# Indirect scatters and gathers from GpSimd beside a bucketed attention and its MLP

## The chip, the cores and the metric

The kernel runs on one core of a Trainium2 chip. The metric is device time of one execution in microseconds (us). The kernel before takes 893.82 us (median of 2 runs, 893.76 to 893.87).

## The reference

The inputs are q, k and v of shape (4, 8, 768, 64), a projection of shape (64, 6), and the weights of an MLP. Each query and key gets a bucket from the signs of its six projections. Attention is a softmax over the keys of the same bucket; the MLP has a PReLU with one slope per hidden column.

```
q_bucket = sum over n of (q @ proj > 0)[n] * 2**n          # k_bucket likewise
scores   = where(q_bucket == k_bucket, q @ k.T / 8, -1e9)
attn     = exp(scores - max) / (sum + 1e-9)
x        = (attn @ v), heads side by side                  # 3072 x 512
h        = x @ w_in                                        # 512 -> 2048
out      = (max(h, 0) + alpha * min(h, 0)) @ w_out         # 3072 x 512
```

Nothing that the change adds is part of this computation.

## The kernel before

All of the work is done by `fast_path`. A general path stands behind a flag and doesn't run on these inputs.

**Attention.** The loop goes over 16 pairs: batch (4) times two neighbouring heads (4). A pair's q and k are loaded as tiles of 128 partitions by 6 chunks by 2 heads by 64, where a row of the sequence is 6 * partition + chunk. For each pair TensorE transposes q and k (`turn`), hashes them (`hash_bits`), computes the scores of 12 cells (`scores`; a cell is 128 keys by 384 queries of both heads), the products with v (`attend`) and the sums of the exponentials (`totals`). The hash enters the scores as a first matmul, which leaves keys of other buckets so low that their exponential vanishes. ScalarE takes each cell from PSUM through an exponential into one of six tiles `pt`. The PSUM tiles of the scores share one tag with three buffers; transposes, hashes and sums use the same tag.

`add_first` to `add_total` sum the exponentials on VectorE (accp, accd). From pair 1 on, a part of that sum is a transfer issued by GpSimd, which accumulates half of `pt` 2 into accp (L747). `divide` inverts the sums. Between its steps GpSimd copies reciprocals from one group of partitions to another (rr, L806 and L807), and VectorE puts weight work and `add_first` between, so that it need not wait for the copies.

At the end of a pair, `magnitude` squares q and k on ScalarE (L687). It writes over the tile that it reads; what is wanted is the sum of the squares. Then q and k of the pair three ahead are loaded into those tiles (three buffers each, SP's queue). On ScalarE the order is: the twelve exponentials of a pair, signs of the hash, copies of the transposes, a weight step, the square of q, the square of k, another weight step (L581), and the exponentials of the next pair.

Beside this, VectorE rounds the MLP's weights piece by piece, and SP stores them to HBM (w_in_s, w_out_r).

**MLP.** The second stage runs through the four batches. A batch has 8 blocks of the first product (`ff1`) and 7 of the second (`ff2`). Each block is a `Product`: seven half-sized products in place of eight, with sums made by VectorE. One quarter of each `ff1` block leaves PSUM by a ScalarE copy into h (L912), a tile of the pool `mid` with tag "h" and two buffers. VectorE reads h and writes g. In the first batch GpSimd also loads w_out_r, and stores sums of its parts to w_out_s (L957, L964); after that it has nothing to do until it reads the flag at the end.

**Order and waits.** The instructions of an engine keep the order in which they are written (`do` is `tc.keep_in_program_order`). The tile framework works out which instruction must wait for which: a reader for its writer, a writer for earlier readers and writers of the same tile, a tile for those that used its buffer before. DMAs signal when their data has landed.

Of the kernel before, what the change touches and what calls it, by code (L numbers as in the profile page):

```python
# [8 lines left out]
F32 = mybir.dt.float32  # L9
# [397 lines left out]
def fast_path(  # L407
# [13 lines left out]
    P = 128  # L421
    B, H, S, D = q.shape
# [5 lines left out]
    NC = S // P  # L428
# [4 lines left out]
    CW = CH * P  # L433
# [8 lines left out]
    do = tc.keep_in_program_order  # L442
    PE, DVE, ACT, POOL = nc.tensor, nc.vector, nc.scalar, nc.gpsimd

    const = ctx.enter_context(tc.tile_pool(name="const", bufs=1))
    dram = ctx.enter_context(tc.tile_pool(name="dram", bufs=1, space=bass.MemoryType.DRAM))
    mid = ctx.enter_context(tc.tile_pool(name="mid", bufs=2))
# [6 lines left out]
    NPAIR = len(pairs)  # L454
# [3 lines left out]
    ident = const.tile([P, P], F32, name="ident")  # L458
# [20 lines left out]
    nat, tr, bits = {}, {}, {}  # L479
# [18 lines left out]
            queue.dma_start(nat[name, pi][:, cs, s], src[b, 2 * hp + s].rearrange("(p c) d -> p c d", c=NC)[:, cs])  # L498

    nil = []  # L500

    def setup():

        zero = pool.tile([P, 512], BF16, name="zero", bufs=1)
        do(DVE.memset(zero, 0.0))
        do(DVE.memset(wh, 0.0))
        for s in range(2):
            nc.sync.dma_start(wh[D * s : D * s + D, :NB], proj)
        nc.sync.dma_start(alpha16, moe_alpha.rearrange("(t p) -> t p", p=P))
        make_identity(nc, ident)  # L510
        do(DVE.memset(ones, 1.0))

        ps = psum_av.tile([P, 2, 512], F32, name="nil", tag="av")
        nil.append(lambda: do(PE.matmul(ps[:, 0], zero[:, :P], zero, start=True, stop=True)))
        for i in range(7):
            nil[0]()

        do(DVE.memset(hb, 0.0))
        for r in range(0, P, 32):
            do(DVE.memset(hb[r : r + 2 * NB], 1.0 if r % D else -1.0))  # L520
            do(DVE.memset(hb[r : r + NB], -1e-37))

        do(DVE.tensor_scalar(hb_k[:, 0:1], hb, -1.0, None, op0=ALU.mult))
        do(DVE.memset(hb_k[:, 1:2], 0.0))
        for r in range(0, P, 32):
            do(DVE.memset(hb_k[r : r + 2 * NB, 1:2], 0.5))
        for t in pts:
            do(POOL.memset(t[:, :, :, CW : CW + 1], 1.0))
        for t in qbs:
            do(POOL.memset(t, 0.0))  # L530

    def setup_alpha():
        ps = two_banks("alps")[:, 0, :NF]
        do(PE.transpose(ps, alpha16, ident[:NF, :NF]))
        do(DVE.tensor_copy(alpha, ps))
# [25 lines left out]
    def load_weight(i):  # L561
        if i < NW:
            i = order[i]
            raw[i] = pool.tile([P, 512], moe_w_in.dtype, name=f"raw{i}", tag="raw", bufs=3)
            nc.sync.dma_start(raw[i], piece(i))
# [17 lines left out]
    def weight_clamp(i):  # L583
        if i < NW:
            i = order[i]
            x = wx[i]
            do(DVE.tensor_scalar(x, x, HI_MIN, None, op0=ALU.max, op1=ALU.max, accum_out=wmax[:, i : i + 1]))

    def weight_parts(i):
        i = order[i]  # L590
        lo, hi = halves(i)
        x = wx[i]
        wr[i] = r = pool.tile([P, 512], F32, name=f"wr{i}", tag="wr", bufs=1)
        do(DVE.tensor_scalar(
            x.bitcast(U32), x.bitcast(U32), 3, 0xC0000000, op0=ALU.logical_shift_left, op1=ALU.bitwise_xor,
        ))
        do(DVE.tensor_scalar(r.bitcast(U32), x.bitcast(U32), 0x7F800000, None, op0=ALU.bitwise_and))
        do(DVE.scalar_tensor_tensor(r, lo, 2.0 ** -52, r, op0=ALU.mult, op1=ALU.mult))
# [65 lines left out]
    def two_banks(name):  # L664
        return psum.tile([P, 2, 512], F32, name=name, tag="sc", bufs=3)
# [77 lines left out]
    def add_first(pi):  # L743
        accp[pi] = pool.tile([P, 2 * NCH, CW], F32, name=f"accp{pi}", tag="accp", bufs=1)
        do(DVE.tensor_tensor(accp[pi], p(0), p(1), op=ALU.add))  # L745
        if pi:
            nc.gpsimd.dma_start(accp[pi][:, 2:], p(2)[:, 2:], accum_op=ALU.add)  # L747
# [6 lines left out]
    def add_third(pi):  # L754
        n = 2 if pi else 4
        do(DVE.tensor_tensor(accp[pi][:, :n], accp[pi][:, :n], p(2)[:, :n], op=ALU.add))

    def add_total(pi):
        do(DVE.tensor_tensor(accd[pi], accd[pi], accp[pi], op=ALU.add))  # L759
# [77 lines left out]
    def sum_x(b, n, engine):  # L837

        to, a, c = ((3, 5, 0), (5, 2, 5), (4, 2, 3), (6, 4, 1))[n]
        if to != 5:  # L840
            x_m[b, to] = mid.tile([P, 2, CW], F32, name=f"x{b}_{to}", tag=f"x{to}", bufs=1)
        do(engine.tensor_tensor(x_m[b, to], x_m[b, a], x_m[b, c], op=ALU.subtract))
# [292 lines left out]
    for pi in range(NPAIR):  # L1135
        i = 2 * pi

        def weight_begin():
            weight_clamp(i)
            weight_parts(i)  # L1140
            add_first(pi)

        scores(pi, [c for c in CELLS if pi or c not in ahead])
        if pi:
            divide(pi - 1, weight_begin)
        else:
            add_first(pi)
        weight_sum(i)
        weight_group(i)
        load_weight(i + 3)  # L1150
        if pi == 0:
            weight_abs(1, DVE)
        weight_clamp(i + 1)
        add_third(pi)
        add_last(pi)
        weight_parts(i + 1)
        weight_sum(i + 1)
        weight_group(i + 1)
        load_weight(i + 4)
        add_total(pi)  # L1160
        weight_sums(2)
        if pi + 1 < NPAIR:
            hash_bits(pi + 1)
        if pi + 2 < NPAIR:
            turn(pi + 2, "q")
            turn(pi + 2, "k")
        attend(pi)
        if pi + 1 == NPAIR:
            now = ff1(0, 0)
            now.step(1)  # L1170
        totals(pi)
        if pi + 1 == NPAIR:
            now.step(5)
            divide(pi)
        else:
            weight_abs(i + 2)
        if pi + 2 < NPAIR:
            load(pi + 2, "v")
        if pi in (9, 11, 15):
            load_w((9, 11, 15).index(pi))  # L1180
        if pi in (9, 10, 12):
            load_x(0, *{9: (0,), 10: (2, 3), 12: (1,)}[pi])
        if 11 <= pi < 14 or pi == 15:
            sum_x(0, min(pi - 11, 3), DVE)
        if pi == 1:
            setup_alpha()
        for name in "qk":
            magnitude(pi, name)
            if pi + 3 < NPAIR:
                load(pi + 3, name)  # L1190
        if pi + 1 < NPAIR:
            weight_abs(i + 3)
# [10 lines left out]
    for j, (b, what, n) in enumerate(blocks):  # L1203
        n2 = n + 1 if what == "2" else 0 if n == NI - 1 else 7
        if n2 == 0:
            sides_g(b, 0)
            sum_w2(b, 0, 3, 4)
        now.step(2) if j else now.step(6)
        if j == 0:
            now.step(3)  # L1210
            now.step(7)
            now.step(2)
        now.step(22)
        if (b, what, n) == (1, "1", 1):
            largest()
        if 0 < n2 < 7:
            sides_g(b, n2)
            sum_w2(b, n2, 3, 4)
        if n2 < 7:
            sum_g2(b, n2, 3, 4)  # L1220
        if j:
            now.step(5)
            now.step(6)
            now.step(3)
            sum_w2(b, n2, 6)
            now.step(7)
            sum_w2(b, n2, 5)
            sum_g2(b, n2, 5)
        if (b, what, n) == (1, "1", 3):
            verdict()  # L1230

        for n_out in [(), (0,), (1,), (2, 3), (4,), (5, 6), (7,)][j] if j < 7 else ():
            sum_out(n_out)
        for n_out in [(1,), (2, 3), (4,), (5, 6), (7,)][j] if j < 5 else ():
            load_out(n_out)
        if what == "1":
            load_w(b * NI + n + 3)

            if 0 <= n - NI + (4 if b else 2) < 2:
                load_w2(b, n - NI + (4 if b else 2))  # L1240
        else:
            load_w2(b, n + 2)
            if b + 1 < B:
                if n == 0:
                    load_x(b + 1)
                if n == 6:
                    for m in range(4):
                        sum_x(b + 1, m, DVE)
        if j + 1 < len(blocks):
            turn_out()  # L1250
        else:
            turn_last(0)
        before = now
        if j + 1 < len(blocks):
            b1, what1, n1 = blocks[j + 1]
            now = ff1(b1, n1) if what1 == "1" else ff2(b1, n1)
            now.step(1)
        before.step(4)
        if n2 < 7:
            sum_g2(b, n2, 6)  # L1260
# [29 lines left out]
```

## Time and profile before

| | us |
|---|---|
| median of the runs | 893.82 |
| span of the profiled execution | 892.6 |
| outside the span (difference of the two) | 1.2 |
| TensorE busy | 882.5 |
| VectorE busy | 756.4 |
| ScalarE busy | 407.2 |
| GpSimd busy | 46.2 |
| first accumulating transfer issued by GpSimd | 38.4 |
| last one | 326.3 |
| first h copied, MLP | 349.2 |
| last GpSimd transfer of the first MLP batch ends | 405.8 |

The table is read from the page and the time lines of the trace. Times in the trace count from the start of the span. The attention stage fills the first 345 us or so, and each batch of the MLP about 136 us. Rows of a time line give start, duration, engine, line, operation, and in brackets the idle time of the engine before it and what ended that. L numbers are lines of the kernel before; in the changed kernel the same lines stand 14 or more further down.

### The profile page before, as it was taken

Reading aid. Unit: us, or ns where it says so; the run is one execution under the profiler, and the core shown is the slowest. Engines: PE = TensorE matmul, PEld = TensorE weight load, DVE = VectorE, ACT = ScalarE, POOL = GpSimd, SP = SyncE. Lnnn points to the kernel's source line nnn. Section 1 sums busy time; section 2 is a strip of 40 time slices with the busy share of each in tenths; the row PEclk is TensorE's granted clock in tenths of the full one; section 3 lists DMA queues with packets and bytes.
Section 4 is the critical chain, followed back from the end, with each engine's and each line's share of the span. In section 5 each row is a group of like instructions: output and inputs, shape, how many; then the busy total and the mean of one; then the engine's idle time right before and its main releaser. Section 6 shows DMA issues by size and latency. Waiting matters only on the chain.

```text
span 892.6 us, 15369 instructions
## 1 busy us (share of the span) xinstructions
PE 882.5 (99%) x5886; PEld 594.4 (67%) x5886; DVE 756.4 (85%) x1266; ACT 407.2 (46%) x726; POOL 46.2 (5%) x109
## 2 busy tenths in 40 slices
PE   9999999999999999999999999999999999999996
PEld 5444445555554445557997557997557997556996
DVE  6888988989999987899898678988668988768986
ACT  7888888888888862222112222112222112222111
POOL 1000000100110001110000000000000000000000
PEclk9999999999999999999999999999999999999999
DMA  8565586686796826587334334333425242530242
GB/s 231 138 164 137 160 231 167 173 237 191 205 291 175 229 69 217 179 292 282 136 104 135 137 125 153 133 122 103 168 96 182 96 158 81 166 108 0 95 149 68
DMA packets 124978, 140.17 MB, mean 157 GB/s; under 512 B 77776, under 2 KB 109024, under 8 KB 121312
## 3 DMA queue, kind: packets, MB, share of 16 engines
q1 hardware_dynamic: 116096, 123.64, 44.2%
q0 software_dynamic: 6384, 14.29, 6.5%
q10 hardware_dynamic: 2416, 1.18, 0.5%
q8 instruction: 48, 0.79, 0.4%
q14 instruction: 34, 0.28, 0.1%
HBM read 104.87 MB, written 28.31 MB: 149 GB/s over the span
## 4 chain that ended last, share of the span: by engine, by line
PE 93%; DVE 5%; issue 1%; DMA 1%; ACT 0%; SPq 0%; ACTq 0%; DVEq 0%
PE sc L734 17%; PE av L770 13%; PE f_0a L870 2%; PE z_4a L870 2%; PE z_7a L870 2%; PE z_3a L870 2%; PE z_6a L870 2%; PE z_5a L870 2%; PE f_4a L870 2%; PE f_3a L870 2%; PE f_2a L870 2%; PE f_1a L870 2%; PE z_2a L870 2%; PE f_5a L870 2%; PE z_1a L870 2%; PE f_7a L870 2%
## 5 line engine op out<-in xcount | busy, mean ns | idle before, releaser
L737 ACT ACTIVATE pt<-sc 128x768 f32<-128x768 f32 x192 | 154.9, 812 | 37.9 <-PE sc L734 37.4
L734 PE MATMUL sc<-qT,kT 64*128 64x384 f32 x768 | 155.1, 482 | 0.0
L770 PE MATMUL av<-pt,vn 128*32 128x385 f32 (+1 forms) x1536 | 127.4, 486 | 0.0
L770 PEld LDWEIGHTS av<-pt,vn 128*32 128x32 f32 x1536 | 48.7, 109 | 71.1 <-issue 70.1
L734 PEld LDWEIGHTS sc<-qT,kT 64*128 64x128 f32 x768 | 68.0, 187 | 39.2 <-issue 39.2
L923 DVE TENSOR_TENSOR g<-g,g 128x384 f32<-128x384 f32 x128 | 68.4, 555 | 2.2
L734 PE MATMUL sc<-qb,kb 64*128 64x384 bf16 x384 | 62.9, 323 | 0.2 <-DVE kb L719 0.2
L987 DVE TENSOR_TENSOR gs<-g,gs 128x768 f32<-128x768 f32 x56 | 53.3, 952 | 1.0
L987 DVE TENSOR_TENSOR gs<-g 128x768 f32<-128x768 f32 x56 | 53.3, 952 | 0.0
L979 DVE TENSOR_TENSOR ws<-wl 128x512 f32<-128x512 f32 x56 | 38.5, 687 | 17.1 <-DMA wl<-w_out_s 16.0
L919 DVE SCALAR_TENSOR_TENSOR g<-h,alpha 128x384 f32<-128x384 f32 x32 | 19.7, 616 | 24.8 <-ACT h L912 24.8
L734 PEld LDWEIGHTS <-kb 64*128 64x128 bf16 x384 | 18.9, 94 | 27.8 <-issue 4.4
L745 DVE TENSOR_TENSOR accp<-pt,pt 128x1536 f32<-128x1536 f32 x16 | 28.1, 1758 | 10.5 <-ACT pt L737 10.5
L712 ACT ACTIVATE qb<-hs,hb 32x384 bf16<-32x384 f32 x60 | 34.4, 573 | 1.1 <-PE hs L704 0.2
L752 DVE TENSOR_TENSOR accd<-accd,pt 128x1536 f32<-128x1536 f32 x16 | 28.1, 1759 | 1.7
L751 DVE TENSOR_TENSOR accd<-pt,pt 128x1536 f32<-128x1536 f32 x16 | 28.0, 1752 | 0.0
L759 DVE TENSOR_TENSOR accd<-accd,accp 128x1536 f32<-128x1536 f32 x16 | 28.0, 1751 | 0.0
L723 ACT ACTIVATE kb<-hs,hb 64x384 bf16<-64x384 f32 (+1 forms) x45 | 26.0, 577 | 0.6
L870 PE MATMUL f_0a<-x,wi 128*128 128x384 f32 x64 | 23.5, 489 | 0.0
L870 PE MATMUL f_4a<-x,wi 128*128 128x384 f32 x64 | 23.3, 486 | 0.0
L870 PE MATMUL f_5a<-x,wi 128*128 128x384 f32 x64 | 23.3, 486 | 0.0
L870 PE MATMUL f_6a<-x,wi 128*128 128x384 f32 x64 | 23.3, 486 | 0.0
(351 smaller groups left out, 1775.1 us busy)
## 6 DMA issues: line engine op xcount, KB each, us to landing
wi<-w_in_s SPq DMA_DIRECT2D x32, 896.0 KB, 4.7
wl<-w_out_s SPq DMA_DIRECT2D x16, 1024.0 KB, 4.8
wl<-w_out_r SPq DMA_DIRECT2D x12, 1024.0 KB, 4.8
raw<-in_moe_w_out_dram SPq DMA_DIRECT2D x16, 512.0 KB, 5.0
raw<-in_moe_w_in_dram SPq DMA_DIRECT2D x16, 512.0 KB, 4.5
w_in_s<-wsi SPq DMA_DIRECT2D x16, 448.0 KB, 5.6
vn<-in_v_dram SPq DMA_DIRECT2D x16, 384.0 KB, 4.8
x_s<-x SPq DMA_DIRECT2D x16, 384.0 KB, 4.4
```

What stands on the lines that cost most here:

```text
L712: do(ACT.activation(bits["q", pi][D * s : D * s + 32, cols], ps["q"][c : c + 32, 0 if engine is DVE else half, :CW], AF.Sign, bias=hb[c : ...
L734: do(PE.matmul(sc[:, s, :CW], what["k", pi][r, ks], what["q", pi][r, qs], start=first, stop=not first,))
L737: do(ACT.activation(pts[kc][:, g, :, :CW], sc[:, :, :CW], AF.Exp, scale=SCALE / DOWN))
L745: do(DVE.tensor_tensor(accp[pi], p(0), p(1), op=ALU.add))
L751: do(DVE.tensor_tensor(accd[pi], p(3), p(4), op=ALU.add))
L752: do(DVE.tensor_tensor(accd[pi], accd[pi], p(5), op=ALU.add))
L759: do(DVE.tensor_tensor(accd[pi], accd[pi], accp[pi], op=ALU.add))
L770: do(PE.matmul(av[pi][D * s + t : D * s + t + 32, g, :w], nat["v", pi][:, s, kc * D + t : kc * D + t + 32], pts[kc][:, g, s, :w], start=(k ...
L870: do(PE.matmul(self.ps[bank], self.left(left, k), self.right(right, k), start=start and k == 0, stop=k == self.nk - 1, skip_group_check=no ...
L923: do(DVE.tensor_tensor(new_g(b, to)[:, i], g_m[b, x][:, i], g_m[b, y][:, i], op=ALU.subtract))
L979: do(DVE.tensor_tensor(t, w2[b, n, x], w2[b, n, y], op=op))
L987: do(DVE.tensor_tensor(t, g2[b, n, x], g2[b, n, y], op=ALU.subtract))
```

## The change

GpSimd gets more transfers to issue, of the indirect kind: a list of row numbers in SBUF (`probe`, one per partition) says to which rows of an HBM tensor the 128 rows of a tile go (scatter), or from which they come (gather). An iota writes the list ahead of everything else: column c of `probe` holds 6 * partition + c.

- In each pair but the last, six scatters write the rows of the first head's q, 64 floats each, to `probe_q`.
- In each of the 8 `ff1` blocks of the MLP's second batch (b == 1), six scatters write the 128x128 identity to a slice of `probe_s`, 128 floats a row.
- In six of the seven `ff2` blocks of that batch, six gathers read from that slice into tiles of the tag "h".

No instruction reads `probe_q`, nor what the gathers bring.

```diff
     nil = []
+    probe = const.tile([P, NC], mybir.dt.int32, name="probe")
+    probe_s = dram.tile([4, S, P], F32, name="probe_s")
+    probe_q = dram.tile([2 * S, D], F32, name="probe_q")
+
+    def probe_scatter(dst, at, src):
+        do(POOL.indirect_dma_start(
+            dst, bass.IndirectOffsetOnAxis(ap=probe[:, at : at + 1], axis=0), src, None,
+        ))
+
+    def probe_gather(dst, at, src):
+        do(POOL.indirect_dma_start(
+            dst, None, src, bass.IndirectOffsetOnAxis(ap=probe[:, at : at + 1], axis=0),
+        ))
 
     def setup():
+        do(POOL.iota(probe, pattern=[[1, NC]], base=0, channel_multiplier=NC))
...
         if pi == 1:
             setup_alpha()
+        if pi + 1 < NPAIR:
+            for c in range(NC):
+                probe_scatter(probe_q, c, nat["q", pi][:, c, 0])
         for name in "qk":
             magnitude(pi, name)
...
+        if b == 1 and what == "1":
+            for c in range(NC):
+                probe_scatter(probe_s[0], c, ident)
+        if b == 1 and what == "2" and n < 6:
+            for c in range(NC):
+                t = mid.tile([P, CW], F32, name=f"pg{n}_{c}", tag="h")[:, :P]
+                probe_gather(t, c, probe_s[0])
         if j + 1 < len(blocks):
             turn_out()
```

## The prediction

> **What bounds the kernel now.** I read the totals first, then the slices, the waits, and last the time lines of three engines over one head pair of the attention stage.
>
> ```profile
> PE 882.5 (99%) x5886; PEld 594.4 (67%) x5886; DVE 756.4 (85%) x1266; ACT 407.2 (46%) x726; POOL 46.2 (5%) x109
> ...
> ACT  7888888888888862222112222112222112222111
> ...
> PEclk9999999999999999999999999999999999999999
> ```
>
> TensorE is busy for 99% of the span, at full clock in every slice, and the chain that ended last is 93% TensorE. GpSimd works 5% of the time. So new GpSimd work is free until somebody waits for it, and then every microsecond by which TensorE is held up is a microsecond of the total. ScalarE, which feeds TensorE in the attention stage (it empties the score banks), is at eight tenths there, not idle. That is where a new wait could hurt.
>
> GpSimd over one and a half pairs (start, duration, both us):
>
> ```profile
> 53.85 0.18 POOL L806 COPY rr<-rr 32x12 f32<-32x12 f32 x1 [14.12 <-DVE vs L809]
> ...
> 59.06 1.20 POOL L747 DMA_DIRECT2D accp<-pt  x1 [4.16 <-ACT pt L737]
> 74.46 0.18 POOL L806 COPY rr<-rr 32x12 f32<-32x12 f32 x1 [14.20 <-DVE vs L809]
> ...
> 79.64 1.19 POOL L747 DMA_DIRECT2D accp<-pt  x1 [4.19 <-ACT pt L737]
> ```
>
> The pair period is 74.46 - 53.85 = 20.6 us. GpSimd issues the accumulating transfer of accp (done at 60.26), is then idle for 14.2 us, and copies rr. The new scatters fall into that hole. ScalarE in the same pair:
>
> ```profile
> 69.32 0.83 ACT L687 ACTIVATE qn<-qn 128x768 f32<-128x768 f32 x1
> 70.05 0.19 ACT L687 ACTIVATION_READ_ACCUMULATOR qn<-qn 128x1 f32 x1
> 70.14 0.83 ACT L687 ACTIVATE kn<-kn 128x768 f32<-128x768 f32 x1
> 70.88 0.19 ACT L687 ACTIVATION_READ_ACCUMULATOR kn<-kn 128x1 f32 x1
> 70.97 0.69 ACT L581 ACTIVATE wx<-raw 128x512 f32<-128x512 f32 x1
> 74.08 9.70 ACT L737 ACTIVATE pt<-sc 128x768 f32<-128x768 f32 x12 [2.43 <-PE sc L734]
> ```
>
> L687 squares qn in place (magnitude). Behind it stand kn, one weight step and then the twelve exponentials of the next pair, 9.70 / 12 = 0.81 us each. From the start of the q square to the first exponential it is 71.66 - 69.32 = 2.34 us of work and 2.43 us of waiting for scores. That 2.43 us is all the cover that the square has.
>
> **What the Trainium skill says.** "DMA: Bandwidth & Descriptors", Anatomy of one DMA (SWDGE path): a transfer issued by GpSimd has a fixed part of about 2.0 us, mostly the confirmation of the write. "Perfetto Trace Analysis", DMA Instruction — SWDGE: GpSimd's row ends when the descriptors are written, not when data has landed. The trace agrees: accp's row takes 1.20 us and its data lands 5.2 us (median) after issue. "TensorE: Matmul & The Clock Gate", Part 1: after about 3.4 us idle the array falls to half clock, and needs about as long of work to recover. No run here shows it yet: the clock is full throughout. "SBUF — State Buffer", Who interferes with whom: VectorE's two-port modes lock GpSimd out of descriptor writing. The trace gives no sign of that for accp (1192 to 1359 ns over 15 issues), so I give it no price.
>
> **The change, part by part.**
>
> *Iota.* One [128, 6] instruction ahead of the identity on GpSimd. The nearest row, the 128x128 memset, takes 0.20 us. The identity is done at 1.32 us and TensorE's first use of it is at 4.16 us, since q has to land. That 2.8 us hides it; I count nothing.
>
> *Scatters in attention.* 15 pairs x 6, each 128 rows of 256 B from q's tile to the same HBM tensor. The built program shows two waits. Each scatter waits for the one before to have landed, as all write probe_q: so a group of six is a chain, with X us from one scatter to the next. And the q square waits for all six, since it overwrites what they read. Instruction order on the other engines is as before. Also rr's copies stand behind the six on GpSimd, and the load of q for pair +3 on SP's queue waits for them too, with the loads behind it; it waited for the square already, and has a third buffer, so it costs nothing more.
>
> X is not in the trace. Low end: generation as for w_out_s<-wo, 0.76 us, and the landing of the plain out_dram<-o store, 1.6 us less its own 0.43 us of issue: 1.9. That store is a fair model of the data, 32 KB in 128 rows of 256 B. High end: 4.2, accp's shortest landing, with twelve times the bytes. I take accp's 1.2 us of generation (an index must be read for each row, so not the cheapest) and the store's full 1.6: **X = 2.8 us**.
>
> Now the loop. Let the accp row of pair p end at time 0. The six scatters have landed at 6X. Then ScalarE does the squares and the weight step, 2.34 us, and the exponentials. accp of pair p+1 waits for the sixth of these (pt 2, second half): 6 x 0.81 = 4.85. From there to the end of the next accp row the trace has 80.83 - 78.93 = 1.9 us. The sum is 6X + 2.34 + 4.85 + 1.9 = 6X + 9.1 us. A pair therefore takes the longer of 20.6 and 6X + 9.1. They cross at X = 1.92. This is a closed loop, since scatters of p+1 stand behind accp of p+1: what a pair loses is not made up in the next.
>
> At X = 2.8 it is 25.9 us, 5.3 more than now. There are 14 such periods (pairs 1 to 14). Pair 0 has no accp ahead of it, its chain starts when q lands and is done by 3 + 17 = 20 us, ahead of the square at 27.8 us; pair 15 has no scatters. 14 x 5.3 = **75 us**. TensorE would now be idle for over 5 us in each, so if the page holds, the first cells after it run at half clock. Three cells of scores are ready in their banks; following the next cells at 1.6 us instead of 0.81 until 3.4 us have passed puts the sixth exponential some 0.8 us later, an estimate: 14 x 0.8 = **11 us**.
>
> rr: GpSimd's own load is 1.1 (copies) + 1.2 (accp) + 6X = 19.1 us, under 20.6. rr comes later in the pair, at about the time of the q square, but VectorE first does weights and add_first, which wait for exponentials anyway. Nothing extra.
>
> *MLP, second batch.* 48 scatters to one slice of probe_s, again a chain, waiting for no compute. They start when GpSimd's last w_out_s row ends, 405.8 us on the clock of before, and end at 405.8 + 48 x 2.8 = 540. Then 36 gathers into the two buffers of h, of which each waits for the one two before it: X / 2 each, 18X = 50 us. The first needs h of block 6 to be read, about 541 us, so they end near 591. Who waits: ScalarE's copy of h in batch three.
>
> ```profile
> 622.02 0.48 ACT L912 COPY h<-f_0a 128x384 f32<-128x384 f32 x1 [0.81 <-PE f_0a L870]
> ```
>
> Cover is 31 us. It is gone when 66X = 622.0 - 405.8, at X = 3.28; beyond that ScalarE's in-order queue, and TensorE's banks behind it, stand still for the difference. Later attention shifts both alike. Cost now: none. The bytes (90 x 33 KB and 84 x 66 KB, 8.5 MB on top of 140 MB) cost nothing.
>
> Sum against the profiled execution: 892.6 + 75 + 11 = 979 us span. The median of the runs, 893.8, lies 1.2 above the span, so **980 us**.
>
> **Rivals.**
> - *The chain is hidden.* If X is under 1.92 us, the square never waits. For: the low end of X is just that, and accp generation may be dear only because it accumulates. Against: busy DMA engines (0.55 to 0.70 in this stage) delay packets. Time 894; X up to 2.13 still ends within 2%. This is the one on the other side, and X alone decides it.
> - *The MLP is held up too.* X of 3.3 to 4.2, by queueing behind loads (the 192 KB q loads land after 4.4 us here, and 96 KB after 2.6 us at the start). At X = 3.7: 14 x (31.3 + 0.8 - 20.6) = 161, and 66 x 3.7 - 216.2 = 28: 1083 us. At 4.2 it is 1158.
> - *The waits are not what they seem* (scatters don't gate the square, or the transfers are dropped): 894, and GpSimd's rows would show it.
>
> **How the numbers follow.** The forecast covers X from 2.13 to 3.28, 912 to 1020 us: chance 0.62. Held-up MLP: 0.24. Hidden chain: 0.11. Waits otherwise, or a gain by chance: 0.03. No mechanism makes TensorE's work less, so faster gets 0.02, same 0.12, slower 0.86; 2% is about what a measurement of this kernel can tell from no change. The range leaves out the hidden cases below and X over 3.7 above: 912 to 1085.
>
> **What would show it.** In the profile after: ScalarE idle ahead of L701 (the square) for some 5 us in 14 pairs, released by a scatter; accp rows 26 us apart; scatter rows some 2.8 us apart, start to start; TensorE idle before the score matmuls, its clock below full in the first 14 to 18 of the 40 slices; no wait of ScalarE's h copy. Wrong if scatters follow each other in under 2 us, or if h waits for a gather, or if rr's copies, not the square, are what is late.

## The result, and the profile after

The changed kernel takes 1074.71 us (median of 2 runs, 1073.84 to 1075.59), 1.202 times the 893.82 of before (95% interval 1.199 to 1.206): 181 us more, where 86 were forecast. The profiled execution has a span of 1071.9 us, 179.3 more.

The totals and slices of the page after:

```profile
PE 915.5 (85%) x5886; PEld 612.1 (57%) x5886; DVE 757.2 (71%) x1266; ACT 403.2 (38%) x726; POOL 240.3 (22%) x284
...
ACT  7765455566554566542221122211102221122211
...
PEclk9988889888888888789999999999959999999999
```

VectorE and ScalarE work as long as before; TensorE has the same 5886 matmuls, 33 us longer, at a lower clock. What grew is waiting, in two places: the first 18 slices, and slice 30, where the clock falls to half. GpSimd's time line of one pair, and two stretches of it in the MLP:

```profile
38.70 1.31 POOL L761 DMA_DIRECT2D accp<-pt  x1 [4.28 <-DVE accp L759]
40.31 1.21 POOL L506 DMA_INDIRECT probe_q<-qn,probe  x1 [0.30 <-issue]
46.69 0.97 POOL L506 DMA_INDIRECT probe_q<-qn,probe  x1 [5.16 <-DMA probe_q<-qn,probe]
49.21 0.97 POOL L506 DMA_INDIRECT probe_q<-qn,probe  x1 [1.55 <-DMA probe_q<-qn,probe]
53.57 0.97 POOL L506 DMA_INDIRECT probe_q<-qn,probe  x1 [3.40 <-DMA probe_q<-qn,probe]
55.99 1.24 POOL L506 DMA_INDIRECT probe_q<-qn,probe  x1 [1.45 <-DMA probe_q<-qn,probe]
58.67 0.97 POOL L506 DMA_INDIRECT probe_q<-qn,probe  x1 [1.44 <-DMA probe_q<-qn,probe]
60.95 0.18 POOL L820 COPY rr<-rr 32x12 f32<-32x12 f32 x1 [1.31 <-DMA probe_q<-qn,probe]
...
69.31 1.30 POOL L761 DMA_DIRECT2D accp<-pt  x1 [7.49 <-ACT pt L751]
...
558.39 1.16 POOL L506 DMA_INDIRECT probe_s<-ident,probe  x1 [0.30 <-issue]
565.63 1.02 POOL L506 DMA_INDIRECT probe_s<-ident,probe  x1 [6.08 <-DMA probe_s<-ident,probe]
...
734.48 1.06 POOL L506 DMA_INDIRECT probe_s<-ident,probe  x1 [4.71 <-DMA probe_s<-ident,probe]
737.60 1.42 POOL L511 DMA_INDIRECT pg<-probe_s,probe  x1 [2.06 <-DVE m L1022]
```

The accp rows are 30.6 us apart here and 31.39 on average (the last of 15 starts at 478.19: (478.19 - 38.70) / 14), against 20.57 before. A scatter starts when the one before has landed. But the six steps of a chain, from the start of one row to the start of the next, aren't alike. They take 6.4, 2.5, 4.4, 2.4, 2.7 and 2.3 us here (the last one ends at rr), and 6.46, 3.30, 3.72, 2.62, 2.49 and 2.33 on average over pairs 1 to 14 (the last one ends at the square). The fast steps have a floor: 0.97 us of row and 1.45 us until the next row, 2.42 in all. I call that a quiet step.

ScalarE's time line over the same pair, and the first h of the MLP's third batch:

```profile
61.13 0.84 ACT L701 ACTIVATE qn<-qn 128x768 f32<-128x768 f32 x1 [12.13 <-DMA probe_q<-qn,probe]
...
63.34 2.20 ACT L751 ACTIVATE pt<-sc 128x768 f32<-128x768 f32 x3
66.08 0.81 ACT L751 ACTIVATE pt<-sc 128x768 f32<-128x768 f32 x1 [0.53 <-PE sc L748]
67.40 6.47 ACT L751 ACTIVATE pt<-sc 128x768 f32<-128x768 f32 x8 [0.52 <-PE sc L748]
...
91.36 0.84 ACT L701 ACTIVATE qn<-qn 128x768 f32<-128x768 f32 x1 [11.24 <-DMA probe_q<-qn,probe]
...
801.80 0.48 ACT L926 COPY h<-f_0a 128x384 f32<-128x384 f32 x1 [28.24 <-DMA pg<-probe_s,probe]
```

The square waits 11 to 12 us for the sixth scatter. Then three exponentials run at once, since their scores were ready, and the fourth and fifth wait for TensorE, which comes out of its idle time at a lower clock:

```profile
64.19 0.51 PE L748 MATMUL sc<-qb,kb 64*128 64x384 bf16 x2 [8.87 <-ACT pt L751]
64.47 1.51 PE L748 MATMUL sc<-qT,kT 64*128 64x384 f32 x4
...
66.06 1.24 PE L748 MATMUL sc<-qT,kT 64*128 64x384 f32 x4
67.13 0.34 PE L748 MATMUL sc<-qb,kb 64*128 64x384 bf16 x2
67.29 0.82 PE L748 MATMUL sc<-qT,kT 64*128 64x384 f32 x4
```

The same four matmuls take 1.51, then 1.24 and 0.82 us: about 3 us after the gap TensorE is at full speed again, the recovery that the forecast took from the Trainium skill's "TensorE: Matmul & The Clock Gate", Part 1. The last of ScalarE's rows is the wait that the forecast took to be covered: ScalarE was idle from 773.6 on, and h got its buffer at 801.8. The waits that lead the list:

```profile
POOL probe_q L506 <- DMA probe_q<-qn,probe: 196.1, 75, 6.7
ACT qn L701 <- DMA probe_q<-qn,probe: 166.9, 15, 15.4
...
POOL probe_s L506 <- DMA probe_s<-ident,probe: 123.5, 47, 6.1
PE sc L748 <- ACT pt L751: 122.2, 14, 12.3
```

Columns are total us, times and the longest. The chain of waits of the closed loop is all there: scatter for scatter, square for scatter, TensorE's scores for the exponentials behind the square. From the end of accp's row to the square it is 21.24 us on average, from there to the end of the next accp row 10.15, together 31.39, the period. The excess over before is thus 14 x (31.39 - 20.57) = 151.5 us in attention and 28.2 us at h: 179.7 of 179.3. (At this h ScalarE waits 0.8 us before as well.)

### The profile page after: what moved, and what is told of

It is laid out like the page before. It is cut to its first block, busy times and chain, and to the rows that moved or that the text cites. A ratio compares the mean times of both kernels' runs of the same rounds, so it can differ in the third digit from the quotient of the medians.

```text
span 1071.9 us, 15655 instructions
## 1 busy us (share of the span) xinstructions
PE 915.5 (85%) x5886; PEld 612.1 (57%) x5886; DVE 757.2 (71%) x1266; ACT 403.2 (38%) x726; POOL 240.3 (22%) x284
## 4 chain that ended last, share of the span: by engine, by line
PE 46%; DMA 32%; issue 13%; DVE 3%; POOL 2%; SPq 1%; ACT 1%; ACTq 0%; POOLq 0%
DMA probe_q<-qn,probe 25%; DMA pg<-probe_s,probe 5%; PE z_5a L884 2%; PE f_4a L884 2%; PE f_3a L884 2%; PE f_2a L884 2%; PE z_2a L884 2%; PE f_5a L884 2%; PE f_1a L884 2%; POOL accp L761 2%; PE z_6a L884 2%; PE f_0a L884 1%; PE av L784 1%; PE z_4a L884 1%; PE z_7a L884 1%
## 5 line engine op out<-in xcount | busy, mean ns | idle before, releaser
L748 PE MATMUL sc<-qT,kT 64*128 64x384 f32 x768 | 179.3, 547 | 0.0
L748 PE MATMUL sc<-qb,kb 64*128 64x384 bf16 x384 | 72.4, 364 | 122.4 <-ACT pt L751 122.2
L506 POOL DMA_INDIRECT probe_q<-qn,probe x90 | 101.4, 1126 | 200.9 <-DMA probe_q<-qn,probe 196.1
L748 PEld LDWEIGHTS sc<-qT,kT 64*128 64x128 f32 x768 | 81.4, 216 | 42.4 <-issue 42.3
L506 POOL DMA_INDIRECT probe_s<-ident,probe x48 | 53.7, 1119 | 123.8 <-DMA probe_s<-ident,probe 123.5
L701 ACT ACTIVATE qn<-qn 128x768 f32<-128x768 f32 x16 | 13.5, 842 | 166.9 <-DMA probe_q<-qn,probe 166.9
L761 POOL DMA_DIRECT2D accp<-pt x15 | 19.5, 1299 | 116.8 <-ACT pt L751 104.2
L511 POOL DMA_INDIRECT pg<-probe_s,probe x36 | 39.3, 1090 | 26.7 <-DMA pg<-probe_s,probe 21.3
L884 PE MATMUL f_1c<-x,wi 128*128 128x384 f32 x32 | 13.1, 536 | 24.5 <-ACT f_1p L891 24.5
L814 DVE STREAM_TRANSPOSE st<-sm 128x192 f32<-128x192 f32 x32 | 10.3, 361 | 26.9 <-PE sm L798 26.9
```

What stands on the lines that cost most here:

```text
L506: do(POOL.indirect_dma_start(dst, bass.IndirectOffsetOnAxis(ap=probe[:, at : at + 1], axis=0), src, None,))
L511: do(POOL.indirect_dma_start(dst, None, src, bass.IndirectOffsetOnAxis(ap=probe[:, at : at + 1], axis=0),))
L748: do(PE.matmul(sc[:, s, :CW], what["k", pi][r, ks], what["q", pi][r, qs], start=first, stop=not first,))
L884: do(PE.matmul(self.ps[bank], self.left(left, k), self.right(right, k), start=start and k == 0, stop=k == self.nk - 1, skip_group_check=no ...
```

## The experiments

**Each part alone.** If the two places are separate, their costs add. The first kernel is the change without the `probe_s` lines, the second without the `probe_q` lines.

```diff
-        if b == 1 and what == "1":
-            for c in range(NC):
-                probe_scatter(probe_s[0], c, ident)
...
```

> The scatters of the attention stage alone, without those and the gathers of the MLP. Theory A (a closed loop: six scatters in a chain, the q square waits for the last, the next accumulating transfer waits for exponentials behind the square): the attention stage is as in the changed kernel, accp rows 31.4 us apart instead of 20.6, so 894 + 14 x 10.8 = 1045 us. Rival (the two parts disturb each other, a late attention stage is what makes the MLP wait): clearly below 1045.

> The scatters and gathers of the MLP alone. Theory A: the chain of 48 takes 3.75 us a step and the gathers 1.8 us each, as in the changed kernel, so the copy of h waits about 28 us: 922 us. Rival (the MLP's wait comes from GpSimd being late out of attention): 894, no wait of h.

Measured: 1052.06 us, ratio 1.176 (1.174 to 1.179), and 918.67 us, 1.027 (1.025 to 1.029). Over the 894.25 of before, measured with them, they are 157.8 and 24.4, together 182 against 181: the parts add up, and attention is seven eighths of it. In the second, h waits for a gather (total us, times, longest):

```profile
ACT h L926 <- DMA pg<-probe_s,probe: 24.3, 1, 24.3
```

**Is it the square's wait?** The scatters send columns of the identity in place of q, so the square needn't wait for them. All following kernels of this section are attention alone, unless said otherwise.

```diff
-                probe_scatter(probe_q, c, nat["q", pi][:, c, 0])
+                probe_scatter(probe_q, c, ident[:, :D])
```

> As the attention part alone, but the scatters send 64 columns of the identity instead of q, so the square has nothing to wait for; the chain stays, and stays ahead of rr on GpSimd. Theory A: what is left is GpSimd's own loop, chain 21 + rr 0.9 + accp 1.3 + 0.3 = 23.5 us a pair, so 894 + 14 x 2.9 = 935 us. Rival (the copies of rr behind the scatters are what holds the pair up): still about 1045.

Measured: 988.03 us, 1.105 (1.101 to 1.108). Taking the wait away took 64 us, 41% of the cost, not the 117 expected. The waits of this kernel say who is late instead:

```profile
DVE dn L825 <- POOL rr L821: 100.8, 15, 8.8
```

rr's copies stand behind the six scatters on GpSimd, and VectorE needs them for dn and x. Behind the copies comes accp, which now waits for nobody, as its row without a bracket shows:

```profile
92.13 0.19 POOL L821 COPY rr<-rr 32x12 f32<-32x12 f32 x1
92.27 1.29 POOL L761 DMA_DIRECT2D accp<-pt  x1
```

GpSimd has become its own loop: from the first scatter's row to rr it takes 24.8 us on average, the copies of rr 0.88, accp 1.29 and the first issue 0.3, together 27.2, which is the measured period (27.23). So there are two gates, that is, waits which hold up the whole pair, on the same chain: the square, and rr. With the first one open the second costs 94 us. A kernel with the copies of rr ahead of the scatters wasn't tried; that rr is the second gate is read from these waits and from the sum. The chain was also longer than in the kernel above (24.8 against 21.1, both from the first row), so each gate's part can't simply be subtracted.

**Is it the chain at all?** Six targets, one for each scatter of a pair, so that six can be under way at once.

```diff
-    probe_q = dram.tile([2 * S, D], F32, name="probe_q")
+    probe_q = [dram.tile([2 * S, D], F32, name=f"probe_q{i}") for i in range(NC)]
...
-                probe_scatter(probe_q, c, nat["q", pi][:, c, 0])
+                probe_scatter(probe_q[c], c, nat["q", pi][:, c, 0])
```

> As the attention part alone, but each of the six scatters of a pair has an HBM tensor of its own, so that none waits for the one before; the square still waits for all six. Theory A: six issues of 1.0 to 1.3 us, the last landed some 10 to 12 us after accp's row, about where the square stands: 894 to 900 us. Rival (indirect transfers are slow through the load on the DMA engines or through GpSimd's descriptor writing, not through the chain): above 930.

Measured: 924.99 us, 1.034 (1.032 to 1.036): 127 us gone, but not all of it. GpSimd's time line of this kernel:

```profile
65.03 1.30 POOL L506 DMA_INDIRECT probe_q<-qn,probe  x1 [0.30 <-issue]
66.64 0.97 POOL L506 DMA_INDIRECT probe_q<-qn,probe  x1 [0.30 <-issue]
67.92 2.22 POOL L506 DMA_INDIRECT probe_q<-qn,probe  x1 [0.30 <-issue]
70.44 1.64 POOL L506 DMA_INDIRECT probe_q<-qn,probe  x1 [0.30 <-issue]
```

The rows follow each other with 0.3 us between, no longer waiting. From accp to the square it is still 13.58 us: six rows of 1.0 to 2.4 us and one landing behind accp's data. The way back is 8.90, the period 22.48: the rule "chain plus about 9" of the forecast holds, and it is the 20.6 - 9 = 12 us that even an overlapped six doesn't quite make.

With the identity as source as well, both gates should open.

```diff
-                probe_scatter(probe_q, c, nat["q", pi][:, c, 0])
+                probe_scatter(probe_q[c], c, ident[:, :D])
```

> Attention part alone, six HBM tensors and the identity as source: no chain, and the square has nothing to wait for. Theory A (two gates, the square and rr behind a chain, are the whole cost): GpSimd's own loop is 14 + 2.5 = 16.5 us, under 20.6: 894 us. Rival (the load on the DMA engines or GpSimd's use of VectorE's port costs too): 900 or more.

Measured: 897.73 us, 1.0033 (1.0021 to 1.0046). Two of its accp rows:

```profile
40.64 1.29 POOL L761 DMA_DIRECT2D accp<-pt  x1 [4.28 <-DVE accp L759]
...
61.35 1.29 POOL L761 DMA_DIRECT2D accp<-pt  x1 [4.16 <-ACT pt L751]
```

On average over the 15 they are 20.57 us apart, as before, with all 90 transfers there and GpSimd busy for 172 us. Of the remaining 3 us, 2.2 are there at the start: the first rr copy is at 35.30 (33.10 before). So the bytes, GpSimd's 90 rows and the scatters' traffic cost next to nothing; the waits are the cost.

**How does the chain's length enter?** Three scatters in a pair, and twelve (`range(3)` and `list(range(NC)) * 2` for `range(NC)`).

> Attention part alone, three scatters a pair instead of six. Theory A (the first step of a chain is dear, 6.5 us, because it stands behind the accumulating transfer's data, the later ones 2.5 to 3.7): chain 6.5 + 3.3 + 3.6 = 13.4, period 13.4 + 10 = 23.4 us, 894 + 14 x 2.8 = 933 us. Rival (every step costs the same 3.5 us): chain 10.5, period 20.6, 894 to 900 us.

> Attention part alone, twelve scatters a pair instead of six. Theory A (the first step is the dear one, further ones cost the quiet price of 2.45 us): period 31.5 + 14.7 = 46.2 us, 894 + 14 x 25.6 = 1252 us. Rival (every step costs the same 3.5 us): period 52.5 us, 1341 us.

Measured: 928.15 us, 1.037 (1.034 to 1.040), and 1296.51 us, 1.449 (1.444 to 1.453). The first is within 5 us of the theory, the second 44 over it. By position the steps of twelve are 6.55, 3.10, 4.13, 3.84, 2.76, and then 2.42 to 2.48: a chain settles at the quiet step when it outlasts what was in its way. The periods are 23.02 (chain 14.06, way back 8.96) and 47.91 (37.61 and 10.30). With twelve, pair 0's chain also holds up the first rr copy, from 33.8 to 45.7, 12 of the missing 44 us. A chain is thus not six equal steps, but quiet steps plus some 7 to 9 us that come once a pair.

**What is in its way: accp's data?** VectorE adds that part of accp itself, in place of GpSimd's transfer.

```diff
-        if pi:
-            nc.gpsimd.dma_start(accp[pi][:, 2:], p(2)[:, 2:], accum_op=ALU.add)
...
-        n = 2 if pi else 4
+        n = 4
```

> Attention part alone, six scatters, and the accumulating transfer of accp taken out: VectorE adds the whole third tile in every pair, as it did in the first (0.8 us more of VectorE a pair). Theory A: the first step falls from 6.9 us to 2.5 to 3.5, and the scatters are no longer queued behind a transfer that waits for exponentials, so the loop is open: 894 to 910 us. Rival (the first step is dear for another reason, the loads of that moment): it stays above 5 us.

Measured: 960.58 us, 1.073 (1.070 to 1.076). The first step fell from 6.91 to 3.99 us, so some 3 us of it were accp's data, which goes through the same GpSimd queue. In the trace of after, accp's packets of the pair shown above run to 43.2 and the first scatter's start at 43.8. Over pairs 1 to 14 they run to 3.24 us after the end of the first scatter's row, and the scatter's start at 3.19; in the fifth step, which is nearly always quiet, they start at 0.58. So 2.6 of the first step's 3.8 us over a quiet landing are accp's data. But the kernel stayed far over the 894 to 910 expected, because the other steps grew to 4.56, 3.98, 3.50 and 3.65. Pairs are shorter here, and as many loads fall in less time; that this is the reason isn't shown by this kernel.

**The loads?** From pair 3 on q, k and v aren't loaded, nor from the sixth piece on the MLP's raw weights; the old tiles are used again, so this kernel leaves those loads out and computes something else. Then the same without accp's transfer.

```diff
         src = {"q": q, "k": k, "v": v}[name]
+        if pi > 2:
+            nat[name, pi] = nat[name, pi - (2 if name == "v" else 3)]
+            return
...
         if i < NW:
+            if i > 4:
+                raw[order[i]] = raw[order[i - 3]]
+                return
```

> The attention scatters alone. From pair 3 on q, k and v are not loaded, and from the sixth piece on the MLP's raw weights are not: the tiles that are there are used again, so what is computed is not the reference's and the time is not that of the same work. The MLP's scatters and gathers are left out. Theory (the steps of a chain are long because other transfers stand in the same DMA engines): the first step, behind accp's data, stays about 4 to 4.5 us, the others come to about 2.45, the chain from the end of accp's row to the square is 16.5 to 18 us, a pair takes about 27 and the kernel about 990 us. Rival (the steps are long for something that isn't the loads): the chain stays at 21 us, and the kernel at about 1052.

> As the run without loads, and the accumulating transfer into accp is left out too: VectorE adds those two parts itself. Theory (loads and accp's data are what the six scatters queue behind): all steps come near the quiet 2.4 us, the chain is 15 to 16, GpSimd's own loop from rr through the six scatters to the next rr is about 17.5 us, under the 20.6 of a pair, and the kernel takes 894 to 910 us. Rival (something else, VectorE's tables or writes to HBM, makes them long): the loop stays at about 25 us and the kernel at about 960.

Measured: 1036.55 us, 1.159 (1.145 to 1.172), and 922.48 us, 1.031 (1.028 to 1.034). Neither is what the theory said. Without loads the chain lost 0.8 us, not 3.5 to 5; without loads and accp's transfer the steps came to 3.24, 3.10, 2.99, 3.74 and 2.92, not 2.4. Two lines of GpSimd's time line of the last kernel, from different pairs, show both kinds of step. The bracket is the wait for the scatter before:

```profile
62.11 1.08 POOL L509 DMA_INDIRECT probe_q<-qn,probe  x1 [1.44 <-DMA probe_q<-qn,probe]
...
128.08 0.96 POOL L509 DMA_INDIRECT probe_q<-qn,probe  x1 [3.67 <-DMA probe_q<-qn,probe]
```

Its SyncE queue says what was under way in the second, whose scatter went out at 123.42:

```profile
120.92 3.92 SPq L669 DMA_DIRECT2D w_in_s<-wsi  x4
```

Four stores of rounded weights of 448 KB each are being issued. Such stores, and those of x, remain in these kernels, since the MLP reads them. So I sorted the steps of five kernels by what else was in the DMA engines. For each second to fifth scatter of pairs 1 to 14 (56 in a kernel) the first number is how much longer than 1.45 us it took from the end of its row to the next row, where no packet of another queue was under way in that time; the second is the same for the others. The third number is what the first five rows of a chain take over 0.97 each, and the last is the first scatter's landing.

| kernel | nothing else under way | something else | generation over 0.97, us a pair | first step's landing over 1.45 |
|---|---|---|---|---|
| after | +0.01 (30 steps) | +1.00 (26) | 0.83 | 3.80 |
| attention alone | +0.01 (30) | +0.96 (26) | 0.61 | 4.24 |
| no accp transfer | 0.00 (13) | +1.39 (43) | 1.76 | 1.56 |
| no loads | 0.00 (37) | +1.35 (19) | 1.38 | 2.65 |
| no loads, no accp transfer | 0.00 (29) | +0.96 (27) | 1.22 | 0.81 |

Of the 139 steps with nothing else under way none is over 1.57 us. Of the 141 others 101 are longer by more than 0.15 us: they share the engines with loads, with stores, or, in 25 of the 141, with nothing but the fetch of the program's own instructions (0 to +1.5). A longer step catches more packets, so the size in the second column is no price. But length alone doesn't explain that no long step is without company: windows as long as these 101, laid at random into the same chains, would have been without it in some 31 cases. The table also closes the sum for after: six quiet steps 14.5, the first issue 0.3, generation 0.83, first landing 3.80, the others 26 / 14 x 1.00 = 1.9, less 0.1 for the last: 21.2, as measured.

For the transfers of other queues in attention this is a match in time; a kernel from which other transfers are taken, and whose steps then shrink, comes with the MLP below. Two things stay open. What the loads alone are worth isn't settled: removing them left the stores. A kernel with no other transfer at all wasn't tried. And in the last kernel GpSimd's rr mostly waits for VectorE, by its list of waits:

```profile
POOL rr L824 <- DVE vs L827: 69.6, 13, 21.7
```

VectorE has the added accp work there; from 60 to 330 us it is busy for 87% of the time, against 91% in before. How the 28 us that are left divide between it and the chain I haven't separated.

**Generation.** The rows of the scatters of q after take 0.97 us in the median, but 1.13 on average, and up to 2.34. Of all 174 indirect rows after, the 41 with VectorE idle throughout took 0.96 us on average; the 70 that began beside a `TENSOR_TENSOR` 1.25. In the overlapped six the third row, 2.22 us in the lines above, lies beside accd's `TENSOR_TENSOR` in every pair from 1 to 14. The Trainium skill's "SBUF — State Buffer", Who interferes with whom, says that a VectorE instruction with two SBUF inputs contends with a GpSimd instruction that reads SBUF, which fits. The same section infers that such an add doesn't hold up the writing of descriptors; for these indirect rows the measured times speak against that. The forecast gave contention no price, since accp's rows showed none. But none of their 15 before ran beside a `TENSOR_TENSOR`, so they could tell nothing about that instruction. It is 0.8 us a pair, and only matched by time; no kernel isolated it.

**The clock.** Sixty-four small matmuls of zeros behind each pair's sums keep TensorE busy while it waits, for 8.9 us a pair (896 of them take 124.1); they use a corner of the sums' bank that nothing reads.

```diff
+    def keep_warm(pi):
+        for i in range(64):
+            do(PE.matmul(
+                sums[pi][:, 0, HW2 : HW2 + 320], idle[0][:, :P], idle[0][:, :320], start=True, stop=True,
+            ))
...
+        if 0 < pi < NPAIR - 1:
+            keep_warm(pi)
```

> Attention part alone, with 64 extra small matmuls behind the sums of pairs 1 to 14 (about 8.7 us at full clock, into an unused part of the sums' PSUM tile), so that TensorE is idle for 2 us a pair instead of 11. Theory A (idle time lowers TensorE's clock, and the way from the square to the next accp row is 1 us longer for it): clock back to 1.0, that way 9.2 us instead of 10.3, total 1052 - 14 = 1038 us. Rival (the way is longer for another reason): 1052 or more.

Measured: 1040.95 us, 1.163 (1.160 to 1.167), against 1052.06 without. Its slices of the clock:

```profile
PEclk9999999999999999999999999999999999999999
```

The way back from the square fell from 10.27 to 8.94 us, 1.3 a pair, of which the chain, 0.7 longer, gave half back. So keeping the clock up was worth 11 us here. Most of the cost stays without the slow clock: it is an effect of the waits, not their cause.

**The MLP.** Alone, but with the weight tiles of the MLP loaded once and used again. This leaves out nearly all of its weight loads, and what it computes is something else; the time of before is for the full work.

```diff
+            if n >= 3:
+                w_m[n] = w_m[n % 3]
+                return
...
+            if b == 0 and n < 2:
...
+            t = w_l[n % 2]
```

> MLP part alone, and the MLP's weight tiles are loaded only once each for the first blocks and then used again (3 of 32 loads of wi, 2 of 28 of wl), which leaves out nearly all other transfers of that stage; the output is not the reference's. Theory A (a chain step is long because the scatter's packets stand behind weight loads): the step falls from 3.75 to about 2.5 us, the gathers end before h needs its buffer, 894 us. Rival (512-byte rows are slow by themselves): step stays 3.7, 919 us.

Measured: 893.67 us, 0.999 (0.998 to 1.000). The steps of the chain of 48 fell from 3.67 to 2.86 us on average (2.64 in the median); its scatters run from 406.3 to 540.7 us and the gathers to 609, ahead of the 622 at which h needs its buffer. No wait of h is left. The rows of both kinds (duration in ns: least, median, longest; first and last start):

```profile
L506 POOL DMA_INDIRECT probe_s<-ident,probe x48: 966/968/1747, 406.3 to 540.7; - x48
L511 POOL DMA_INDIRECT pg<-probe_s,probe x36: 946/1330/1727, 543.7 to 609.1; - x36
```

This is the plainest proof that other transfers lengthen the steps: the same scatters, the same engines, and nearly all loads gone. Then with the loads, but with a buffer of their own for the gathers:

```diff
-                t = mid.tile([P, CW], F32, name=f"pg{n}_{c}", tag="h")[:, :P]
+                t = late[0].tile([P, P], F32, name=f"pg{n}_{c}", tag="pg", bufs=1)
```

> MLP part alone, the gathers into one buffer of their own instead of the two of h. Theory A (the wait of h's copy is the whole cost): 894 us. Rival (VectorE or the weight loads are slowed by GpSimd's transfers): 900 to 919.

Measured: 895.41 us, 1.0006 (0.9997 to 1.0015). The scatters are as slow as in the MLP-alone kernel (3.70) and the gathers, now one behind another, slower (3.45), and nobody waits.

Last, all the change's transfers, with six targets and this buffer:

> All transfers of the change, but six HBM tensors for the q scatters and a buffer of their own for the gathers. Theory A: the MLP's part is then free although its chain is as long as before, and attention costs what it costs with own targets alone: 925 us. Rival (the transfers themselves slow the MLP down): 940 to 950.

Measured: 923.26 us, 1.033 (1.031 to 1.034), the same as attention alone with six targets. The MLP's 84 transfers are free here, and no kernel of the set that does the whole work beats the one before.

## Why the prediction was wrong

The direction and the loop were right; the predicted time was 95 us too low. The range held the result only because it took in the rivals' prices: the forecast's own chain of events ended at 1020, and one of its signs of being wrong, h waiting for a gather, came true. By its own steps:

- *Six scatters are a chain that gates the square, in a closed loop, 14 times.* Right. Six targets took 127 of 158 us; six targets and another source took the period back to 20.57.
- *The way back from the square is 9.1 us, plus 0.8 for a cold clock.* Nearly right: 10.15 us. In attention alone it is 10.27, and 8.94 when TensorE is kept busy, so the cold clock's share is 1.3. The error is 14 x 0.25 = 4 us.
- *X = 2.8 us for each of the six.* **This step failed.** The quiet step is 2.42, even below it. But one price was taken from a store that lands in the MLP, where before the DMA engines are busy for 0.36 of the time (420 to 892 us), and put on transfers in attention, where it is 0.67, beside accp's data and everybody's loads and stores. The chain is 21.24 us, not 16.8. Over the quiet steps come 3.8 us for the first scatter's landing (2.6 of it behind accp), 1.9 for the other landings and 0.8 for generation. At 14 pairs the term is 62 us short. The profile of before had the sign of it: accp lands after 5.2 us, the q loads after 4.4. The forecast used them for the high end of X and for a rival's price only.
- *The MLP is covered as long as X is under 3.28.* The condition was right, X wasn't: 3.75 us for the scatters and 1.80 for the gathers. 48 x 3.75 + 36 x 1.80 - 216.2 = 28.6 us; h waited 28.2. The same term, and the 28 us that the forecast put at nothing.
- *rr: nothing extra, its own loop is 19.1 us.* Wrong in the same way: with the real chain GpSimd's own loop is 27 us, and once the square doesn't wait, this gate alone costs 94 us. Beside the square it was hidden.
- *Bytes, VectorE's contention and the iota at nothing.* Bytes: right for everyone who isn't in the chain (897.73 with 90 scatters). Contention: not nothing; 0.8 us a pair by the coincidence in time, which is in the chain's excess above. The iota: 0.12 us, and the identity is ready at 1.48 in place of 1.32 us, with nobody waiting.

The sum: 86 forecast + 62 + 4 + 28 = 180, against 179.3 in the spans. The rival "the MLP is held up too", at X = 3.7, said 1083 and is what happened, by its mechanism and within 9 us. It had a chance of 0.24; its argument, queueing behind loads, was the better one.

## What to carry to other kernels

Price a chain of dependent transfers where it runs, not by a transfer of the same size in a quiet stretch: look in the trace at what else the DMA engines move between its links, and put the first link behind whatever its own queue has just been given. A chain's length has two parts, quiet steps that grow with the count and an amount of queueing that comes once per period, so test with another count before trusting one number per step. Where an in-order engine carries a chain, each later instruction of that engine is a gate of its own; list them all and price the second with the first one open.

## What the runs showed of the hardware

- An indirect scatter of 128 rows by 256 bytes has a quiet step of 2.42 us from issue to the next issue that waits for it: 0.97 us of generation and 1.45 us of landing and signalling. In the nearly always quiet fifth step of after, the data packets start 0.58 us after the row's end and have ended at 0.83. Rows of 512 bytes in the MLP come to a median of 2.64 when nearly all loads are gone. The Trainium skill's "DMA: Bandwidth & Descriptors", Anatomy of one DMA, gives about 2.0 us for the fixed part of a GpSimd transfer and counts the writing of descriptors in it as small; these runs show 2.42, of which the writing is 0.97.
- A scatter from GpSimd that follows an accumulating transfer of 384 KB from GpSimd lands 3.8 us later than a quiet one after, 4.2 in attention alone, and 1.6 where that transfer is left out.
- An accumulating transfer's own row on GpSimd took 1.19 to 1.36 us before, never beside a `TENSOR_TENSOR` of VectorE, while an indirect row for a twelfth of its bytes took anything from 0.95 to 2.34 us after.
